# Linear attention and a gated MLP in one kernel: idle products at the start, a held-back turning of q, and tile 0's second layer in another order

## The chip, the core and the metric

The kernel runs on one core of a Trainium2 chip. The metric is the device time of one execution in microseconds (us), lower is better. Each kernel was run three times; the median is shown. Beside those runs stands one execution with the hardware profiler on, whose trace is what is read below.

## The reference

Inputs are q, k, v of shape (8 batches, 8 heads, 576 positions, 64), a norm vector g of 64, w_in (512 x 2048) and w_out (2048 x 512), all float32. The output has 4608 x 512 float32.

```
kv  = einsum('bhsd,bhse->bhde', k, v)
out = einsum('bhsd,bhde->bhse', q, kv)
x   = out / sqrt(mean(out*out, -1) + 1e-6) * g_norm     # attention without softmax, then a norm per head
x   = x.transpose(0, 2, 1, 3).reshape(4608, 512)
h   = x @ w_in
g   = h * (1 / (1 + exp(-1.702 * h)))
y   = g @ w_out
```

## The kernel before, in words

**Tiles.** Each batch gives one tile of 512 rows (positions 0 to 511 of it, or, for the first two batches, 512 of its 576 rows in another numbering). The 64 rows that are left of each batch are collected in `x_rem` and form a ninth tile. The loop at the end of the kernel runs t = 0 to 8: tile t goes through the first layer (x times w_in, with the gate on ScalarE) and the second layer (times w_out), and into the products of tile t the attention of batch t + 1 is woven. `at1(n, ...)` and `at2(n, ...)` put a piece of work behind step n of the tile's first or second layer. Order on every engine is written out by hand (`manual_schedule`); nothing is moved by a scheduler, and every wait follows from the data and the buffers.

**Start.** Before the loop batch 0's attention is done pair of heads by pair of heads (`First`): q turned by TensorE (`q`, 12 narrow products), `kv` (12 narrow products), `out`, `ss` (sum of squares by a product with ones), then a root on ScalarE and `apply` on VectorE. `busy(n)` (L865) issues n products of 128 x 512 into a bank that nobody reads; before, it stands 12, 2 and 2 times among the first pairs. Then tile 0's first layer runs plainly (L473): first the columns 0 to 3 for the parts of w_in, then columns 8 and 9, 10 and 11, 4, 5, 6 and so on (`COLS`).

**Loads.** All loads that change float32 to float16 go through POOL's queue, in the order of the program: k, q, v of batch 0, w_in in eight pieces, then w_out mixed with batch 1's q, k, v (L920 to L930), later batch 2's q (`load_q`), batch 2's k, v in two halves (`load_kv`), and so on. A load is issued only when the load eight places ahead of it in this queue has landed (there are eight semaphores, used in turn), and when the buffer that it writes has been read.

**Tile 0's second layer** (`project_all`, L811) is 64 products of 128 x 512 into four banks o, one for each 128 rows (mo), over 16 row blocks of w_out (fo); two of the banks belong to the first layer's pool of three (`ps_h`). Its list `steps` says which (mo, fo) comes when, and batch 1's attention (`Second`) is woven in by `at2` numbers: q, kv, out, ss, apply for four pairs c. `Second` takes its ss banks from `ps_h`.

**Tiles 1 to 8** use seven products in place of eight for each 2 x 2 block (L584 in the first layer, L704 in the second). This takes sums of weights, made once by VectorE: `w_in_sums` into `ws`, and `weight_sum(n, i0, i1)` (L606) into `tw`, the part n of w_out's sums for row blocks i0 to i1. Products 5, 6, 7 and 4 of the second layer read tw's parts 0, 1, 2 and 3. Sums of the activations go into `xS` and `gS`.

**Turning.** From batch 2 on q and x are turned by DMA, issued from SP's queue: `transpose_q` (qTd, L290), `transpose_rest` (qTr, L294), and two for x (L368). SP's queue also carries the stores of the output: `store_early` (L838), eight stores, for tiles 0 and 1. Before, tile 0's eight stores come first, then batch 2's q.

Of the kernel before, what the change touches and what calls it, by code (L numbers as in the profile page):

```python
# [16 lines left out]
def kernel(  # L17
# [10 lines left out]
    nc = tc.nc  # L28

    B, H, S, D = q.shape  # L30
# [11 lines left out]
    EARLY = 2  # L42
# [47 lines left out]
    def early_load(n, b, c0, c1):  # L90
        nc.gpsimd.dma_start(
            out=raw[n][0:PE_, c0:c1, :].rearrange("p c (l x) -> p (c l) x", l=2),
            in_=early_src(n, b, c0, c1),
        )
# [15 lines left out]
    RS = H * RW  # L110
# [26 lines left out]
    def q_rows(b):  # L137

        rows = qbuf if b % 2 else qraw.rearrange("p c x -> p (c x)")
        return rows[:, 0 : H * J * D]  # L140
# [64 lines left out]
    def load_w_out(f0, f1):  # L205
        nc.gpsimd.dma_start(
            out=w_out_sb[:, f0:f1, :],
            in_=moe_w_out[f0 * P : f1 * P, :].rearrange("(fo ki) n -> ki fo n", ki=P),
        )
# [11 lines left out]
    class Attention:  # L221
# [63 lines left out]
                    r = slice(hl * D, (hl + 1) * D)  # L285
                    copy(self.engine, self.kb[to, c0:c1, half, 1 - hl], self.kvp[r, c0:c1, :])

        def transpose_q(self):
            self.qTd = attn.tile([P, H * J // 2, P], F16, name="qTd", tag="qTd", bufs=1)
            nc.sync.dma_start_transpose(out=self.qTd, in_=q_rows(self.b))  # L290

        def transpose_rest(self):
# [489 lines left out]
    def layers(t, units1, units2):  # L782
        hid = d0 if t == 0 else Hidden(t)
        seven = Seven(t, hid.gT) if t else None
        left = hid_seven(t, hid, seven, units1) if t else first_columns(hid, units1)
        osbs[t] = opool.tile([P, 4, DM], F32, name="osb", tag="osb")
        if t:
            todo = {n: [lambda x=x: seven.sums(*x) for x in xs] for n, xs in plan(t).later.items()}
            for n, us in units2.items():
                todo.setdefault(n, []).extend(us)  # L790
            for n, us in left.items():
                todo[n] = us + todo.get(n, [])
            seven.run(todo)
        else:
            project_all(hid.gT, units2)
        if t < EARLY:
            store_early(t)
        elif t < B and t not in HALVED:
            store(t, 0, J)

    def first_columns(hid, units):
# [9 lines left out]
    def project_all(gT, units):  # L811

        os = {}

        def project(mo, fo):
            if fo == 0:
                pool, tag = (ps_h, "hT") if mo < 2 else (ps_o, "o")
                os[mo] = pool.tile([P, DM], F32, name="o", tag=tag)
            nc.tensor.matmul(  # L819
                os[mo],  # L820
                gT[:, fo, mo * P : (mo + 1) * P],
                w_out_sb[:, fo, :],
                start=(fo == 0),
                stop=(fo == FO - 1),
            )
            if fo == FO - 1:
                copy = nc.scalar.copy if mo % 2 else nc.vector.tensor_copy
                copy(osbs[0][:, mo, :], os[mo])

        steps = [(mo, 4 * i + k) for i in range(3) for mo in range(4) for k in range(4)]  # L830
        steps += [(mo, f + k) for f in (12, 14) for mo in range(2) for k in range(2)]
        steps += [(mo, 12 + k) for mo in (2, 3) for k in range(4)]
        for n, (mo, fo) in enumerate(steps):
            project(mo, fo)
            for u in units.get(n, ()):
                u()
# [52 lines left out]
    a0.ss(0)  # L889
    a0.out(1)  # L890
    a0.q(2)
    a0.kv(2)
    a0.ss(1)
    a0.apply(0)
# [1 line left out]
    a0.q(3)  # L896
    a0.apply(1)
    d0 = Hidden(0)
    a0.kv(3)
    a0.ss(2)  # L900
    a0.apply(2)
# [22 lines left out]
    load_w_out(8, 10)  # L924
    load_w_out(10, 12)
    early_load("v", 1, 0, 2)
    load_w_out(12, 14)
    early_load("k", 1, 2, NPAIR)
    early_load("v", 1, 2, NPAIR)
    load_w_out(14, FO)  # L930

    made = {}
# [49 lines left out]
    for t in range(NT):  # L982
        b = t + 1
        u1, u2 = {}, {}

        def at1(i, f, *args):
            u1.setdefault(i, []).append(lambda: f(*args))

        def at2(i, f, *args):
            u2.setdefault(i, []).append(lambda: f(*args))  # L990

        def of(b, name, *args):
            return lambda: getattr(live[b], name)(*args)

        if t == 0:
            for l in range(2):
                at1(6, nc.vector.memset, kvd[l], 0.0)
            at1(7, of(0, "out", NPAIR))
            at1(7, scale_w_in, 0, 4)
            at1(7, w_in_sums, 0, 2)  # L1000
            at1(8, start, 1)
            at1(12, scale_w_in, 4, 6)
            at1(12, w_in_sums, 2, 3)
            at1(13, load_q, 2)
            at2(4, setattr, a0, "ss_pool", Attention.ss_pool)
            at2(4, of(0, "ss", NPAIR, True))
            at2(4, of(0, "apply", NPAIR))
            at2(18, weight_sum, 0, 0, HF)
            at2(18, scale_w_in, 6, 8)
            at2(18, w_in_sums, 3, 4)  # L1010
            for c in range(NPAIR):
                at1(12, of(1, "pack_q", c))
                at2(9 + 3 * c, of(1, "q", c))
                at2((36, 36, 49, 49)[c], of(1, "kv", c))
                at2((41, 43, 54, 55)[c], of(1, "out", c))
                at2((45, 50, 58, 60)[c], of(1, "ss", c))
                at2((48, 52, 58, 62)[c], of(1, "apply", c))
            for n in range(1, 4):
                at2(19, weight_sum, n, 0, 4)
                at2(38, weight_sum, n, 4, 6)  # L1020
            at2(39, load_kv, 2, 0, H // 2, False)
            at2(51, clear_rest)
            at2(51, load_kv, 2, H // 2, H)

            def first_sum():
                made[1] = Sums(1, xT[1])
                made[1].form(0)

            at2(55, first_sum)
        elif b < B:  # L1030
            todo = plan(t)
            at = todo.attn
            if t == 1:
                at1(todo.steps.index("kv"), of(b, "kv_all", "D"))
                at1(5, start, b)
                at1(5, of(b, "transpose_q"))
                at1(5, of(b, "transpose_rest"))
                at1(4, nc.scalar.preload_act_table_set, "gelu_apprx_sigmoid_and_others")
                for n, i in ((1, 8), (2, 11), (3, 16)):
                    at1(i, weight_sum, n, 6, HF)  # L1040
                at1(22, load_kv, 3)
                at1(22, load_q, 3)
                at2(88, start, 3)
                at2(88, of(3, "kv_all", "A"))
                at2(89, load_kv, 4)
                at2(89, load_q, 4)
            elif t + 2 < B:
                at2(at["rows"][0], start, t + 2)
                at2(at["rows"][0], of(t + 2, "kv_products"))
                at2(52, of(t + 2, "kv_copies", "A"))  # L1050
                if t + 3 < B:
                    at2(at["rows"][0], load_kv, t + 3, 0, H, False, "k")
                    at2(101, after_turn, b)
                    at2(101, load_kv, t + 3, 0, H, True, "v")
                    at2(101, after_queries, t + 2)
                    at2(101, load_q, t + 3)
            if t + 2 < B:
                at2(49 if t > 1 else 100, of(t + 2, "transpose_q"))
                at2(100, of(t + 2, "transpose_rest"))
            at2(at["table"], nc.scalar.preload_act_table_set, "abs_reciprocal_sqrt_and_small")  # L1060
            for h in range(2):
                at2(at["roots"][h], of(b, "roots", h))
            for j in range(J):
                if j < J // 2:
                    at2(at["rows"][j], of(b, "rows", j))
                for name in ("add_up", "turn"):
                    at2(at[name][j], of(b, name, j))
            rest = (80, 90, 96, 97) if 1 < t < B - 2 else (46, 74, 80, 82)
            at2(rest[0], of(b, "out", NPAIR))
            at2(rest[1], of(b, "ss", NPAIR))  # L1070
            at2(rest[2], of(b, "apply", NPAIR))
            at2(rest[3], nc.scalar.preload_act_table_set, "gelu_apprx_sigmoid_and_others")
        elif t < B:
            for name in ("ss_pool", "rest_pool"):
                at2(16, setattr, live[1], name, (ps_a, "att"))
            at2(16, of(1, "out", NPAIR))
            at2(34, nc.scalar.preload_act_table_set, "abs_reciprocal_sqrt_and_small")
            at2(44, of(1, "ss", NPAIR))
            at2(50, of(1, "apply", NPAIR))
            at2(52, nc.scalar.preload_act_table_set, "gelu_apprx_sigmoid_and_others")  # L1080
        layers(t, u1, u2)


# [28 lines left out]
```

## Time and profile before

| what | value |
|---|---|
| median of 3 runs | 259.11 us (258.8 to 259.48) |
| the profiled execution | 259.74 us, of which its span is 258.0 |
| mean granted TensorE clock of that execution | 0.993 |
| TensorE busy (products) | 251.7 us, 98% |
| VectorE busy | 193.9 us, 75% |
| ScalarE busy | 177.1 us, 69% |
| POOL busy (without issuing loads) | 57.0 us, 22% |
| POOL's queue of loads | 18.31 MB, 55.3% of 16 engines' time |
| SP's and ACT's queue | 16.29 MB, 27.4% |

How to read it: the span is from the first to the last recorded instruction; the time of the execution has some 1.7 us around it. PE is TensorE, PEld its loading of weights (which overlaps the products), DVE is VectorE, ACT ScalarE, POOL GpSimd, SP the engine that only issues transfers. A timeline row gives start and length in us, engine, line, operation, what is written and read, shapes, and the count of instructions merged in it; in brackets stands the idle time ahead of it and what ended that. The lengths of products overlap: a row's end lies about 0.17 us behind the start of what follows it without a gap, so distances are taken from start to start. "DMA to landing" is from a transfer's issue to its last byte. A kernel line such as L704 names the call that recorded the instruction, which may be a helper that many places use. In the changed file the lines from 290 on lie two to some ten further down.

### The profile page before, as it was taken

How to read it: one execution, taken by the hardware profiler on the slowest of the kernel's cores; microseconds unless marked ns; L12 is line 12 of the kernel's file. 1: busy time of each engine (PE TensorE's matmuls, PEld its weight loads, DVE VectorE, ACT ScalarE, POOL GpSimd, SP SyncE). 2: the span in 40 equal slices, each digit the busy share in tenths (PEclk: the TensorE clock that was granted, in tenths of full speed). 3: DMA queues.
4: the chain of work that ended last, by engine and by line, in shares of the span. 5: the costliest groups of instructions: out<-in, count | busy, mean ns of one | idle time of the engine just before them, and what ended most of it. 6: DMA issues, size and time to landing. Idle time of an engine off the chain costs nothing.

```text
span 258.0 us, 6355 instructions
## 1 busy us (share of the span) xinstructions
PE 251.7 (98%) x2596; PEld 204.4 (79%) x2596; DVE 193.9 (75%) x344; ACT 177.1 (69%) x322; POOL 57.0 (22%) x92
## 2 busy tenths in 40 slices
PE   8899999999999999999999999999999999999994
PEld 2444454788888888888888888898888888888883
DVE  1546685899958986798679867987799787857872
ACT  3458743988758894899579957995799469536800
POOL 8773244208061013301150134000000000000013
PEclk9979999999999999999999999999999999999999
DMA  7999999999989979996999699909500430012005
GB/s 181 194 188 206 204 204 197 216 216 115 184 159 208 221 91 224 153 158 81 186 184 164 84 205 135 190 5 136 202 4 0 84 163 3 0 57 108 3 19 145
DMA packets 68687, 35.33 MB, mean 137 GB/s; under 512 B 37970, under 2 KB 66258, under 8 KB 68402
## 3 DMA queue, kind: packets, MB, share of 16 engines
q0 software_dynamic: 37632, 18.31, 55.3%
q1 hardware_dynamic: 30624, 16.29, 27.4%
q8 instruction: 20, 0.33, 0.5%
q10 hardware_dynamic: 402, 0.33, 0.5%
q14 instruction: 9, 0.07, 0.1%
HBM read 36.70 MB, written 9.44 MB: 179 GB/s over the span
## 4 chain that ended last, share of the span: by engine, by line
PE 93%; DMA 4%; issue 0%; POOL 0%; DVE 0%
PE o L704 38%; PE h L584 38%; PE hT L473 6%; PE o L819 5%; DMA vbuf<-in_v_dram 2%; DMA qraw<-in_q_dram 2%; PE kvp L247 2%; PE outR L332 1%; PE ss L379 1%; PE outT L302 1%; PE q L454 0%; PE kvp L259 0%; PE outT L306 0%; PE kv L259 0%; DVE osb L684 0%
## 5 line engine op out<-in xcount | busy, mean ns | idle before, releaser
L561 ACT ACTIVATE gT<-h 128x512 f16<-128x512 f32 x96 | 52.5, 601 | 5.6 <-PE h L584 5.6
L584 PEld LDWEIGHTS <-ws 128*128 128x128 f16 x512 | 50.1, 98 | 5.9
L704 PEld LDWEIGHTS <-gS 128*128 128x128 f16 x512 | 49.1, 98 | 6.1 <-DVE gS L636 0.3
L584 PE MATMUL h<-xS,ws 128*128 128x256 f16 x384 | 52.2, 273 | 0.0
L704 PE MATMUL o<-tw,gS 128*128 128x256 f16 x384 | 45.6, 273 | 0.0
L584 PEld LDWEIGHTS <-w_in_sb 128*128 128x128 f16 x384 | 37.4, 98 | 4.7
L704 PEld LDWEIGHTS <-gT 128*128 128x128 f16 x384 | 37.6, 98 | 4.3
L704 PE MATMUL o<-w_out_sb,gT 128*128 128x256 f16 x256 | 31.4, 273 | 0.0
L584 PE MATMUL h<-xT,w_in_sb 128*128 128x256 f16 x224 | 31.1, 272 | 0.0
L681 DVE TENSOR_TENSOR osb<-o,qf 128x512 f32<-128x512 f32 (+1 forms) x25 | 16.7, 669 | 11.7 <-PE o L704 11.7
L598 DVE TENSOR_TENSOR h<-h,s 128x512 f32<-128x512 f32 x32 | 22.2, 698 | 4.2 <-PE h L584 2.6
L600 DVE TENSOR_TENSOR s<-h,s 128x512 f32<-128x512 f32 x32 | 22.1, 691 | 4.1 <-PE h L584 3.3
L738 POOL DMA_DIRECT2D out_dram<-osb x6 | 3.2, 537 | 93.2 <-DVE osb L681 93.2
L636 DVE TENSOR_TENSOR gS<-gT 128x512 f16<-128x512 f16 (+2 forms) x32 | 21.3, 685 | 0.6 <-ACT gT L561 0.6
L561 ACT ACTIVATE gT<-s 128x512 f16<-128x512 f32 x32 | 19.8, 628 | 2.4 <-DVE s L600 2.3
L530 DVE COPY s<-h 128x512 f32<-128x512 f32 x19 | 13.0, 686 | 8.2 <-PE h L584 8.2
L584 PE MATMUL h<-xS,w_in_sb 128*128 128x256 f16 x128 | 18.9, 273 | 0.0
L115 POOL DMA_DIRECT2D kraw<-in_k_dram x7 | 6.0, 853 | 56.9 <-PE kvp L247 52.0
L348 DVE TENSOR_REDUCE sum<-sq 128x8 f32<-128x512 f16 x24 | 14.9, 678 | 4.7 <-ACT sq L342 4.7
L320 ACT ACTIVATE sq<-outT 128x512 f16<-128x512 f32 (+1 forms) x16 | 7.9, 495 | 15.1 <-PE outT L302 9.5
L990 ACT ACT_TABLE_LOAD x14 | 18.0, 1283 | 0.2
L381 ACT ACTIVATE rs<-ss,eps_t 128x512 f32<-128x512 f32 (+1 forms) x16 | 9.2, 582 | 12.4 <-PE ss L379 12.3
(104 smaller groups left out, 373.9 us busy)
## 6 DMA issues: line engine op xcount, KB each, us to landing
out_dram<-osb SPq DMA_DIRECT2D x8, 512.0 KB, 4.6
kraw<-in_k_dram POOLq DMA_DIRECT2D x5, 512.0 KB, 6.0
vbuf<-in_v_dram POOLq DMA_DIRECT2D x5, 512.0 KB, 10.4
out_dram<-osb SPq DMA_DIRECT2D x2, 1024.0 KB, 4.9
qraw<-in_q_dram POOLq DMA_DIRECT2D x3, 512.0 KB, 11.6
qbuf<-in_q_dram POOLq DMA_DIRECT2D x3, 512.0 KB, 10.4
out_dram<-osb SPq DMA_DIRECT2D x6, 192.0 KB, 5.9
w_in_sb<-in_moe_w_in_dram POOLq DMA_DIRECT2D x2, 512.0 KB, 10.1
```

The source lines that it names most:

```text
L348: nc.vector.tensor_reduce(out=self.sum4[:, j, :], in_=self.o[j][1].rearrange("p (x d) -> p x d", d=D), op=ALU.add, axis=mybir.AxisListType.X,)
L473: nc.tensor.matmul(self.h[fo], w_in_sb[:, ko, fo * P : (fo + 1) * P], self.x[:, ko], start=(ko == 0), stop=(ko == KO - 1),)
L530: (nc.vector.tensor_copy if engine == "D" else nc.scalar.copy)(to, src)
L561: nc.scalar.activation(self.gT[:, to, n * TH : (n + 1) * TH], src, AFT.Gelu_apprx_sigmoid)
L584: nc.tensor.matmul(bank[name][:, a], w, x, start=(p in (1, 5) and a == 0 and k == 0), stop=(k == KH - 1), skip_group_check=True,)
L598: nc.vector.tensor_add(bank["z"], bank["x"], self.s5)
L600: nc.vector.tensor_add(self.s5, bank["x"], self.s5)
L636: op(s[:, n, lo], a, b)
L681: nc.vector.tensor_add(o, ps, self.kept[with_][:, m])
L704: nc.tensor.matmul(o, a, w, start=(p in (1, 2, 5) and i == 0 and (mo == 0 or split)), stop=(i == HF - 1), skip_group_check=True,)
L819: nc.tensor.matmul(os[mo], gT[:, fo, mo * P : (mo + 1) * P], w_out_sb[:, fo, :], start=(fo == 0), stop=(fo == FO - 1),)
L990: u2.setdefault(i, []).append(lambda: f(*args))
```

## The change

Seven edits, all in the order of work or in which instruction waits for what; the computation is the same.

1. Four more idle products: `busy(1)` ahead of batch 0's third kv and `busy(3)` ahead of its fourth.
2. Batch 1's last k and v are loaded ahead of w_out's row blocks 12 and 13, and these come in two loads in place of one.
3. The end of tile 0's second layer runs row block 12 for all four mo, then 13 for all four, then 14 and 15 for each mo, and batch 1's kv, out, ss, apply stand at other step numbers. From step 57 on, batch 1 takes its ss banks from the other pool (`ps_a`).
4. w_out's sums: parts 1, 2, 3 of row blocks 4 and 5 are no longer made in tile 0's second layer; parts 1 and 2 of blocks 4 to 7 are made in tile 1's first layer, part 3 of blocks 4 to 7 in tile 1's second layer behind product 80.
5. Tile 2's k, v loads stand behind steps 41 and 54 in place of 39 and 51.
6. Turning batch 2's q waits for a copy of one element by POOL, which reads the last piece of batch 2's v (`transpose_q(after=...)`).
7. Tile 0's eight stores are issued behind the turning of batch 2's q, in tile 1's first layer, in place of at the end of tile 0.

```
-        def transpose_q(self):
+        def transpose_q(self, after=None):
             self.qTd = attn.tile([P, H * J // 2, P], F16, name="qTd", tag="qTd", bufs=1)
+            if after is not None:
+                nc.gpsimd.tensor_copy(out=self.qTd[0:1, 0, 0:1], in_=after)
             nc.sync.dma_start_transpose(out=self.qTd, in_=q_rows(self.b))
...
-        if t < EARLY:
+        if t == 1:
             store_early(t)
-        elif t < B and t not in HALVED:
+        elif 1 < t < B and t not in HALVED:
             store(t, 0, J)
...
         steps = [(mo, 4 * i + k) for i in range(3) for mo in range(4) for k in range(4)]
-        steps += [(mo, f + k) for f in (12, 14) for mo in range(2) for k in range(2)]
-        steps += [(mo, 12 + k) for mo in (2, 3) for k in range(4)]
+        steps += [(mo, fo) for fo in (12, 13) for mo in range(4)]
+        steps += [(mo, 14 + k) for mo in range(4) for k in range(2)]
...
     a0.q(2)
+    busy(1)
     a0.kv(2)
...
     d0 = Hidden(0)
+    busy(3)
     a0.kv(3)
...
     early_load("v", 1, 0, 2)
-    load_w_out(12, 14)
     early_load("k", 1, 2, NPAIR)
     early_load("v", 1, 2, NPAIR)
+    load_w_out(12, 13)
+    load_w_out(13, 14)
     load_w_out(14, FO)
...
             at2(4, setattr, a0, "ss_pool", Attention.ss_pool)
+            at2(57, lambda: setattr(live[1], "ss_pool", Attention.ss_pool))
...
-                at2((36, 36, 49, 49)[c], of(1, "kv", c))
-                at2((41, 43, 54, 55)[c], of(1, "out", c))
-                at2((45, 50, 58, 60)[c], of(1, "ss", c))
-                at2((48, 52, 58, 62)[c], of(1, "apply", c))
+                at2((40, 40, 47, 47)[c], of(1, "kv", c))
+                at2((44, 45, 51, 54)[c], of(1, "out", c))
+                at2((47, 48, 56, 58)[c], of(1, "ss", c))
+                at2((50, 52, 57, 60)[c], of(1, "apply", c))
             for n in range(1, 4):
                 at2(19, weight_sum, n, 0, 4)
-                at2(38, weight_sum, n, 4, 6)
-            at2(39, load_kv, 2, 0, H // 2, False)
-            at2(51, clear_rest)
-            at2(51, load_kv, 2, H // 2, H)
+            at2(41, load_kv, 2, 0, H // 2, False)
+            at2(54, clear_rest)
+            at2(54, load_kv, 2, H // 2, H)
...
-                at1(5, of(b, "transpose_q"))
+                at1(5, of(b, "transpose_q", kv_rows["v"][0:1, RS + H * D - 1 : RS + H * D]))
                 at1(5, of(b, "transpose_rest"))
+                at1(5, store_early, 0)
                 at1(4, nc.scalar.preload_act_table_set, "gelu_apprx_sigmoid_and_others")
-                for n, i in ((1, 8), (2, 11), (3, 16)):
-                    at1(i, weight_sum, n, 6, HF)
+                for n, i in ((1, 8), (2, 11)):
+                    at1(i, weight_sum, n, 4, HF)
+                at2(80, weight_sum, 3, 4, HF)
```

## The prediction

> **What bounds the kernel now.** I read the page's chain of waits and clock line first, then TensorE's windows and timeline at the start, then single loads with their time to landing, then the stretches that the change touches.
>
> ```profile
> span 258.0 us, 6355 instructions
> PE 93%; DMA 4%; issue 0%; POOL 0%; DVE 0%
> PEclk9979999999999999999999999999999999999999
> ```
>
> The chain that ended last is TensorE for 93% of the span; the rest is loads ahead of it. The clock line falls in one slice of 40, the third (12.9 to 19.4 us). So only two things can be won: TensorE's waits, and the slow clock of that slice. The windows of TensorE alone (us, busy, granted clock, DMA share, GB/s) cut it finer:
>
> ```profile
> 3.06:6.47 3.41, 3.41 (x9) 1.00 1.13 240
> 6.47:9.88 3.41, 3.03 (x59) 1.00 1.28 190
> 9.88:13.29 3.41, 2.51 (x40) 1.00 1.27 196
> 13.29:16.70 3.41, 3.41 (x20) 0.51 1.31 180
> ```
>
> After a window that was 2.51 of 3.41 us busy comes one at clock 0.51; after 3.03 of 3.41 it did not fall. The DMA share is above 1 throughout: loads set the pace beside TensorE. TensorE's timeline there (start, length, count, wait before it):
>
> ```profile
> 1.28 5.30 PE L867 MATMUL idle<-kvb 128*128 128x512 f16 x12 [1.28 <-DVE one_t L202]
> 9.02 0.45 PE L434 MATMUL q<-ident,qraw 96*64 96x96 f16 x12
> 9.30 0.35 PE L259 MATMUL kv<-vbuf,kraw 96*64 96x64 f16 x12
> 10.54 0.45 PE L434 MATMUL q<-ident,qraw 96*64 96x96 f16 x12
> 11.09 0.38 PE L259 MATMUL kv<-vbuf,kraw 96*64 96x64 f16 x12
> 13.29 0.50 PE L259 MATMUL kv<-vbuf,kraw 96*64 96x64 f16 x12 [0.68 <-DMA vbuf<-in_v_dram]
> 15.40 1.71 PE L473 MATMUL hT<-xT,w_in_sb 128*128 128x512 f16 x4
> 17.17 5.78 PE L473 MATMUL hT<-xT,w_in_sb 128*128 128x512 f16 x26
> 22.90 7.07 PE L473 MATMUL hT<-xT,w_in_sb 128*128 128x512 f16 x32
> 29.81 1.24 PE L819 MATMUL o<-w_out_sb,gT 128*128 128x512 f16 x5
> 47.80 0.60 PE L584 MATMUL h<-xT,w_in_sb 128*128 128x256 f16 x4
> ```
>
> A 512-wide product takes 0.216 us at full clock ((29.81 - 22.90) / 32) and 0.43 when slow (1.71 / 4). From 17.17 on there is hardly a gap.
>
> **Four idle products.** One stands before batch 0's third kv, three before its fourth; 4 x 0.216 = 0.86 us of work. Twelve q products issue in 0.28 (9.02 to 9.30), so the third kv at 11.09 follows a hole of 11.09 - 10.54 - 0.28 = 0.27, and the fourth one of 0.68 or more, in which it waits for v. One product (0.22) and three (0.65) fit in. Their cost is 0; bounds 0 and +0.86, the latter if the loads behind those holes came at once, which nothing here suggests. They raise the window at 9.88 from 2.51 to about 3.2 busy of 3.41, above the 3.03 that kept the clock. I take it that the clock stays.
>
> What that is worth: the fourth kv (0.28) and the 15 wide products after it, up to the first that needs w_in's columns 8 and 9, end at 13.29 + 0.28 + 15 x 0.216 = 16.8, with small waits for w_in's first quarter and a copy 17.0. Before, that product stood at 17.17 + 6 x 0.216 = 18.47 (six of the 26 come ahead of it). So up to 1.45 could be won, but the loads do not move. Two of them, with the third row for the v load:
>
> ```profile
> L180 POOL DMA_DIRECT2D w_in_sb<-in_moe_w_in_dram x1: 747/747/747, 10.5 to 10.5; - x1
> DMA to landing us min/median/max: 7.0/7.0/7.0
> ...
> L180 POOL DMA_DIRECT2D w_in_sb<-in_moe_w_in_dram x1: 747/747/747, 12.8 to 12.8; - x1
> DMA to landing us min/median/max: 9.2/9.2/9.2
> ...
> 7.59 5.57 DMA vbuf<-in_v_dram
> ```
>
> v lands at 13.16 and its product starts 0.13 later (13.29). Columns 8 and 9 land at 17.5, so their product starts at 17.63. Twenty wide products (4.33) and four narrow ones (0.11) later, at 22.07, TensorE wants columns 4 to 7, which land at 12.75 + 9.2 = 21.95, usable at 22.08. Before, it began them at 22.90. **Term: -0.82**; bounds 0 (the clock falls all the same) and -1.45 (the loads come sooner).
>
> A rule of the Trainium skill speaks against this term: "TensorE: Matmul & The Clock Gate", section "Why this matters for your kernels", asks only that no idle gap between bursts exceeds about 3 us. By it the holes of 0.27 and 0.68 would not matter and the term would be 0; the trace disagrees so far, with clock 0.51 behind holes no longer than 0.68.
>
> **Batch 1's loads, steps and w_out.** Tile 0's second layer has the same 64 products. It runs from 29.81 to 47.80, 17.99 us; its work is 64 x 0.216 plus 3.9 of attention products, 17.75, so it holds 0.24 of waits. The rows that set them now and after:
>
> ```profile
> 41.04 1.25 ACT L320 ACTIVATE sq<-outT 128x512 f16<-128x512 f32 x2 [5.15 <-PE outT L302]
> 41.92 0.38 PE L379 MATMUL ss<-sq,ones 128*128 128x512 f16 x1
> 42.33 0.69 ACT L381 ACTIVATE rs<-ss,eps_t 128x512 f32<-128x512 f32 x1
> ...
> L206 POOL DMA_DIRECT2D w_out_sb<-in_moe_w_out_dram x1: 705/705/705, 24.7 to 24.7; - x1
> DMA to landing us min/median/max: 14.6/14.6/14.6
> ...
> L91 POOL DMA_DIRECT2D vbuf<-in_v_dram x1: 673/673/673, 30.1 to 30.1; - x1
> DMA to landing us min/median/max: 11.9/11.9/11.9
> ```
>
> From ss to the end of its root are 42.33 + 0.69 - 41.92 = 1.10. Two first-layer banks are held by rows of o, so batch 1's second ss needs the first's root done; after the change only kv's 0.50 and two products (0.43) stand between the two, so it waits 0.2. The last ss takes a bank of the other pool and does not wait. Waits of 0.2 replace waits of 0.24: **term 0**, bounds -0.2 and +0.4.
>
> The loads: w_out's rows 12 and 13 landed at 24.74 + 14.6 = 39.3 and batch 1's last v at 30.14 + 11.9 = 42.0. With k and v put ahead, each comes 1.3 sooner (the gap that the pair of rows filled) and row 12 lands at about 41.5. TensorE wants the last k, v at 29.0 + 12.7 = 41.7 and row 12 at 42.2, counted from its new start of the layer (29.81 - 0.82). Both are there, by 0.9 and 0.5; if a load slips past, the wait is up to 0.5. POOL's queue issues each load when the one eight places ahead has landed, and splitting the pair of rows adds one place: tile 2's q goes out 0.9 later, but the queue never runs dry, so nothing behind it lands later.
>
> **VectorE's sums and the gS wait.**
>
> ```profile
> 64.21 0.77 PEld L704 LDWEIGHTS <-gS 128*128 128x128 f16 x8 [0.27 <-DVE gS L636]
> ...
> L612 DVE TENSOR_TENSOR tw<-w_out_sb,tw 128x1024 f16<-128x1024 f16 x2 | 1.4, 689 | 0.1
> ```
>
> Six sums of 0.42 become three of 0.69. Two stand in tile 1's first layer (1.38 instead of three of 0.42, 1.26), one in its second layer at product 80, in a hole of VectorE of 1.5 us, and 1.3 ahead of the product that reads it. Batch 1's last two applies end about 1 us earlier against the layer's end, so VectorE comes to gS some 0.15 ahead, and of the wait of 0.27 a part goes: **term -0.08**, bounds -0.15 and +0.15. If VectorE's lead is lost, it pays the extra 0.12 there.
>
> **q's turning and tile 0's stores held back.** A POOL copy now waits for tile 2's last v piece; SP's turning of q waits for the copy, and behind it in SP's queue stand the small turning and tile 0's eight stores, behind these x's turnings of tile 2.
>
> ```profile
> 46.27 4.38 SPq L843 DMA_DIRECT2D out_dram<-osb  x8
> 51.40 4.26 SPq L290 DMA_TRANSPOSE qTd<-qraw  x1
> 63.26 0.64 PE L332 MATMUL outR<-kvd,qTd 64*128 64x64 f16 x32
> 71.86 0.82 PE L247 MATMUL kvp<-vbuf,kraw 128*64 128x64 f16 x40
> ...
> 58.00:60.00 2.00, 2.00 (x20) 1.79 (x19) 1.93 (x6) 1.76 (x4) 1.76 (x2) 1.00 0.09 13
> ...
> L120 POOL DMA_DIRECT2D vbuf<-in_v_dram x1: 691/691/691, 60.8 to 60.8; - x1
> DMA to landing us min/median/max: 7.2/7.2/7.2
> ```
>
> Without the stores' 4.38 among them, tile 2's loads land by about 52; turning starts there, against 51.40, and takes at most 4.26 plus 1.2 for the small one: done by 58, wanted at 63.26 - 0.9. The stores then issue from 56 to 62, partly in the stretch where the DMA share is 0.09 now. The copy holds nothing up on POOL: the load behind it waits for tile 2's kv anyway. Beside the stores run tile 3's k, v, whose last piece landed at 60.8 + 7.2 = 68.0 and is wanted at 71.86: 3.9 to spare. **Term 0**; bounds 0 and +2, worked out below.
>
> **Sum.** -0.82 + 0 + 0 - 0.08 + 0 = -0.90. The profiled execution took 259.74 (span 258.0 and 1.74 around it): 258.84. It is 0.63 above the median of the runs, 259.11, to which I apply the same -0.90: **258.2 us**.
>
> **Rivals.**
> (1) The clock falls as before, because holes this short do not decide it, or the median run never lost what the profiled one did. For it: one window is all that I have, 2.51 against 3.03 busy is a thin bound, the wide products of 1.28 (5.30 / 12 = 0.44 each) were slow for 5 us under full busy, so the clock goes by windows whose place I cannot set; and the runs spread over 258.8 to 259.48, as far as this term. Then only -0.1 to -0.3 is left: 258.9. The Trainium skill (the page named above, section "Part 1: The HAM clock gate") gives a window of 3413 ns that runs free of the kernel's start; the slow stretch of 3.41 agrees.
> (2) The loads come sooner than here, since TensorE's two waits for w_in are all that is left: -1.45 - 0.1, 257.6. Against it: their queue is full from the first microsecond.
> (3) Slower: turning and stores, both moved behind tile 2's loads, meet tile 3's k, v. If those slip by more than 3.9, TensorE stands at the kv of 71.86. The stores alone are 4.38 of issue, and with the 4.26 of turning they are 8.6; halfway between 4.4 and 8.6 the slip is 6.5, some 2 more than is spare after the earlier start: -0.9 + 2 = +1.1, 260.2. Against it: the idle stretch at 58 to 60, and turning that is quicker without loads beside it.
>
> **How the numbers follow.** What a measurement of this kernel can tell from no change is 0.3%, 0.78 us: faster is below 258.33, slower above 259.89. The forecast has 0.57, with a range of its own from 257.9 to 258.6, about 0.47 of it below 258.33 and 0.10 above. Rival 1 has 0.24 (no change), rival 2 0.08 (faster), rival 3 0.11 (slower). So faster 0.55, same 0.34, slower 0.11. The range runs from rival 2's 257.6 to 259.4, which holds rival 1 with the spread of the runs, and leaves out rival 3 and the edges.
>
> **What would show it.** Clock near 1.00 in the window of 13.29 to 16.70; the 26 products split by a wait for w_in before columns 8, and the 32 starting at about 22.1; the second layer starting near 29.0 and lasting 18.0; TensorE's kv of tile 3 at about 71.0 with no wait before it. Wrong if the clock still shows 0.5 there, if w_out's row 12 or batch 1's v ends a wait in the layer, or if the kv near 71 waits for a load.

## The result, and the profile after

The changed kernel is slower: 262.25 us (median of 6 runs, 261.31 to 262.75) against 259.30 us of the kernel before beside it (median of 6, 258.75 to 260.17). The ratio is 1.0107, with a 95% interval from 1.0085 to 1.0129. Ratios here leave out a run that took over 1.5% more than the fastest of its kernel, which are two of the twelve of stores_back and none elsewhere. The prediction said 258.2 us, with a range that ended at 259.4.

The page of the execution profiled after (262.03 us) begins like this; the last two rows are groups of the first layer's products, with their busy time, the mean ns of one, and the idle time before them:

```profile
span 260.2 us, 6364 instructions
PEclk9999999999999999999999999999999999999999
PE 91%; DMA 6%; DVE 1%; SPq 0%; issue 0%; DVEq 0%
L586 PE MATMUL h<-xS,ws 128*128 128x256 f16 x384 | 52.4, 273 | 1.2 <-DVE xS L514 1.1
L586 PE MATMUL h<-xT,w_in_sb 128*128 128x256 f16 x224 | 31.0, 273 | 1.9 <-DMA xT<-x 1.9
```

The dip of the clock line is gone, and yet the span is 2.2 us longer. DMA has grown from 4% to 6% of the chain that ended last, and the first layer's products now wait 1.9 for `xT<-x`, a name that stood in no row of the prediction: x's turning by DMA. The start went better than forecast. First the windows at 9.88 and 13.29, here with all engines (length, then busy time and in brackets the count of PE, PEld, DVE, ACT and POOL, then granted clock, DMA share, GB/s), then TensorE's timeline:

```profile
9.88:13.29 3.41, 3.21 (x43) 1.51 (x43) 2.02 (x5) 2.33 (x4) 2.98 (x5) 1.00 1.28 198
13.29:16.70 3.41, 3.41 (x27) 1.66 (x27) 1.63 (x4) 2.12 (x4) 3.20 (x5) 1.00 1.33 190
```

```profile
10.59 0.39 PE L869 MATMUL idle<-kvb 128*128 128x512 f16 x1
12.56 0.82 PE L869 MATMUL idle<-kvb 128*128 128x512 f16 x3
13.32 0.38 PE L259 MATMUL kv<-vbuf,kraw 96*64 96x64 f16 x12
21.55 7.07 PE L475 MATMUL hT<-xT,w_in_sb 128*128 128x512 f16 x32
28.46 1.24 PE L821 MATMUL o<-w_out_sb,gT 128*128 128x512 f16 x5
46.47 0.60 PE L586 MATMUL h<-xT,w_in_sb 128*128 128x256 f16 x4
...
70.58 0.82 PE L247 MATMUL kvp<-vbuf,kraw 128*64 128x64 f16 x40
72.11 1.91 PE L706 MATMUL o<-tw,gT 128*128 128x256 f16 x16
75.91 1.92 PE L586 MATMUL h<-xT,w_in_sb 128*128 128x256 f16 x16 [1.89 <-DMA xT<-x]
78.97 1.67 PE L586 MATMUL h<-xS,ws 128*128 128x256 f16 x12 [1.13 <-DVE xS L514]
```

The four idle products fit where they were put, and the kv behind them moved by 0.03 (13.29 to 13.32). The 32 products start 1.35 earlier (22.90 to 21.55), tile 0's second layer lasts 18.01 against 17.99, and at tile 3's kv TensorE is still 1.28 ahead (71.86 to 70.58), with no wait there. TensorE's rows of the profile before from there to tile 4's kv, and that kv after:

```profile
73.39 1.91 PE L704 MATMUL o<-tw,gT 128*128 128x256 f16 x16
75.14 1.92 PE L584 MATMUL h<-xT,w_in_sb 128*128 128x256 f16 x16
76.89 1.36 PE L584 MATMUL h<-xS,ws 128*128 128x256 f16 x11
89.21 0.82 PE L247 MATMUL kvp<-vbuf,kraw 128*64 128x64 f16 x40
```

```profile
91.48 0.82 PE L247 MATMUL kvp<-vbuf,kraw 128*64 128x64 f16 x40
```

The lead of 1.28 has become a lag of 2.27 at tile 4's kv. Tile 2's first layer followed the 16 products of 73.39 after 1.75 us; now it follows those of 72.11 after 3.80, and its first products on xS, VectorE's sums of the turned x, come 3.06 behind its start instead of 1.75. That is 2.05 + 1.31 = 3.36 of the 1.28 + 2.27 = 3.55, and both waits hang on the two turnings of x.

SP's queue before the change, with x's turnings for tile 2 and the turning of tile 3's q behind them, and the time of x's turnings to landing:

```profile
68.74 3.26 SPq L368 DMA_TRANSPOSE xT<-x  x2
72.17 1.92 SPq L290 DMA_TRANSPOSE qTd<-qbuf  x1
...
L368 SPq DMA_TRANSPOSE xT<-x x2: 1232/1586/1939, 68.7 to 70.1; - x2
DMA to landing us min/median/max: 4.0/4.2/4.5
```

The same of after, with POOL's copy (edit 6, called the hold from here on). The last rows are the load of tile 3's q, of after and then of before:

```profile
52.49 0.18 POOL L291 COPY qTd<-vbuf 1x1 f16<-1x1 f16 x1 [5.88 <-DMA vbuf<-in_v_dram]
52.70 1.78 SPq L292 DMA_TRANSPOSE qTd<-qraw  x1
56.46 6.34 SPq L845 DMA_DIRECT2D out_dram<-osb  x8
67.46 5.81 SPq L370 DMA_TRANSPOSE xT<-x  x2
...
L370 SPq DMA_TRANSPOSE xT<-x x2: 1267/2856/4446, 67.5 to 68.8; - x2
DMA to landing us min/median/max: 8.4/9.0/9.6
...
L143 POOL DMA_DIRECT2D qbuf<-in_q_dram x1: 902/902/902, 60.5 to 60.5; - x1
DMA to landing us min/median/max: 13.8/13.8/13.8
...
L143 POOL DMA_DIRECT2D qbuf<-in_q_dram x1: 902/902/902, 61.4 to 61.4; - x1
DMA to landing us min/median/max: 9.2/9.2/9.2
```

x's turning is issued 1.28 earlier, as everything is, but takes 8.4 and 9.6 us to land instead of 4.5 and 4.0. Tile 3's k, v, q are loaded from 56.92 on, and the stores of tile 0, 1 MB, now run beside them. The last of the large ones, q, landed at 60.53 + 13.8 = 74.3; before, it was issued at 61.4 and landed after 9.2, at 70.6. So in the new order x's turning has loads beside it until nearly its own end. They are not its only neighbours: the last stores, issued by 62.3, land by 69.4, and tile 4's loads are issued from 71.67, where before they went out at 72.95, when the first turning had all but landed. Windows of before, and below them of after (columns as above), show where room was given up and where it was taken:

```profile
52.00:54.00 2.00, 2.00 (x21) 1.79 (x19) 2.00 (x5) 1.81 (x4) 0.00 (x0) 1.00 1.47 335
72.00:74.00 2.00, 2.00 (x53) 1.82 (x50) 0.49 (x2) 1.44 (x5) 1.05 (x2) 1.00 1.16 255
```

```profile
52.00:54.00 2.00, 2.00 (x20) 1.70 (x19) 2.00 (x5) 1.84 (x4) 0.18 (x1) 1.00 0.01 2
72.00:74.00 2.00, 2.00 (x19) 1.57 (x16) 0.69 (x1) 0.94 (x3) 2.00 (x3) 1.00 1.64 117
74.00:76.00 2.00, 0.11 (x2) 0.09 (x2) 0.00 (x0) 0.59 (x1) 2.00 (x4) 1.00 1.39 160
```

From 52 to 54 the DMA engines now stand nearly still (share 0.01 where it was 1.47): tile 2's last v has landed at 45.93 + 6.5 = 52.4, and q's turning, which the hold lets go at 52.70, moves next to nothing before 54. From 74 to 76 they are busy and TensorE works for 0.11 of 2 us.

### The profile page after: what moved, and what is told of

Same layout as the page of the kernel before. It is cut to its first block, busy times and chain, and to the rows that moved or that the text cites. A ratio compares the mean times of both kernels' runs of the same rounds, so it can differ in the third digit from the quotient of the medians.

```text
span 260.2 us, 6364 instructions
## 1 busy us (share of the span) xinstructions
PE 251.6 (97%) x2600; PEld 204.0 (78%) x2600; DVE 194.3 (75%) x341; ACT 177.1 (68%) x322; POOL 57.5 (22%) x94
## 4 chain that ended last, share of the span: by engine, by line
PE 91%; DMA 6%; DVE 1%; SPq 0%; issue 0%; DVEq 0%
PE h L586 37%; PE o L706 36%; PE hT L475 5%; PE o L821 5%; DMA xT<-x 4%; DMA qf<-in_v_dram 2%; PE kvp L247 1%; PE outR L334 1%; PE ss L381 1%; PE outT L304 1%; PE idle L869 1%; PE q L436 0%; PE kv L259 0%; PE q L456 0%; PE kvp L259 0%; SPq L161 0%
## 5 line engine op out<-in xcount | busy, mean ns | idle before, releaser
L586 PE MATMUL h<-xS,ws 128*128 128x256 f16 x384 | 52.4, 273 | 1.2 <-DVE xS L514 1.1
L532 ACT COPY h<-h 128x512 f32<-128x512 f32 x27 | 15.4, 576 | 4.0 <-PE h L586 3.8
```

The costliest lines, as they stand in the source:

```text
L532: (nc.vector.tensor_copy if engine == "D" else nc.scalar.copy)(to, src)
L586: nc.tensor.matmul(bank[name][:, a], w, x, start=(p in (1, 5) and a == 0 and k == 0), stop=(k == KH - 1), skip_group_check=True,)
```

## The experiments

The main theory was A: the hold and the new place of the stores put the stores beside tile 3's loads, these land later, and x's turning, which then runs beside them, becomes slow. Theory B was that any earlier start of TensorE runs into x's turning. Nine kernels were tried, in three groups; each group had its own runs of the kernel before, with medians of 258.89, 258.88 and 258.92 us.

**stores_back.** The changed kernel with tile 0's stores at the end of tile 0 again, the hold kept.

```
-        if t == 1:
+        if t < EARLY:
             store_early(t)
...
-                at1(5, store_early, 0)
```

> The changed kernel with tile 0's eight stores back at the end of tile 0, ahead of q's turning; the hold on that turning stays. Theory A (the stores, pushed behind the turning to 56.5 to 62.8 us, delay tile 3's k, v and q loads, and x's turning for tile 2 then runs beside these): x's turning lands in 4 to 5 us in place of 8.4 and 9.6, TensorE does not wait at tile 2's start, the span is about 3.3 us below the 260.2 of the changed kernel, and the time about 258.5. Theory B (TensorE is 1.3 us ahead while the transfers are not, so any faster start runs into the turning): a wait of 1 us or more stays there and the time is 259.5 to 260.5.

Measured: 260.18 us (258.77 to 263.21, 12 runs), ratio 1.0038 (1.0010 to 1.0065). In its profile the last load of tile 3, q, lands at 70.9, x's turning takes 6.3 and 7.6, and TensorE waits for VectorE's sums alone, 1.2. Most of the loss goes with the stores; something stays, and differs much from run to run. So theory A's forecast (4 to 5 us, 258.5) was missed, and the time is in theory B's range. The profile shows one likely reason: with the stores beside tile 2's loads, its v lands at 55.5, the hold lets q's turnings go only at 55.71, and these run beside tile 3's loads (issued from 56.78), whose q takes 10.5 to land in place of 9.2.

**no_hold.** The changed kernel without the hold: the stores stay behind q's turnings in SP's queue.

```
-                at1(5, of(b, "transpose_q", kv_rows["v"][0:1, RS + H * D - 1 : RS + H * D]))
+                at1(5, of(b, "transpose_q"))
```

> The changed kernel without the hold: q's turning for batch 2 waits for q alone; the stores still stand behind it. Theory A: turning goes out near 46 us, the stores at about 48 to 54, before tile 3's loads begin at 56.9, and x's turning lands in 4 to 5 us; time about 258.5. Theory C (the stores standing directly ahead of x's turning in SP's queue are what slows it, whenever they are issued): x's turning stays at 7 us or more and the time near 261.5. Theory B: 259.5 to 260.5.

Measured: 258.88 us (258.16 to 259.99), ratio 0.9993 (0.9976 to 1.0009). The stores are issued from 51.88 to 56.6, ahead of tile 3's loads (the last lands by 60, beside them), and no product waits for x's turning (5.3 and 5.8 to landing, where theory A said 4 to 5); one wait of 0.7 is left, for tile 4's v. So it is not the stores' place in the queue, directly ahead of x's turning, that costs (theory C): that place is the same here.

**idle_alone.** The kernel before with the four idle products alone (edit 1).

```
     a0.q(2)
+    busy(1)
     a0.kv(2)
...
     d0 = Hidden(0)
+    busy(3)
     a0.kv(3)
```

> The kernel before with the four idle products and nothing else. Theory A: the clock stays at 1.00 from 13.3 to 16.7 us, the second layer of tile 0 starts 0.8 to 1.35 us earlier, and since nothing else moves the gain is kept: 258.0 to 258.5. Theory B: the layer starts as much earlier, but the gain is lost in a wait for transfers by tile 2's start: 259.0 to 259.5.

Measured: 258.75 us (258.50 to 259.45, 12 runs), ratio 0.9987 (0.9968 to 1.0005): within what can be told from no change. The profile shows the gain of the start in full (the second layer begins at 28.44, against 29.81), and no product waits at tile 2's start, so theory B does not hold here. Yet the median hardly moves. The clocks say why: of the 65 runs of the kernel before in the three groups, only 4, all in the first group, have a mean granted clock of 0.993, the one of the profile that the prediction read; they took 259.40 to 260.18. The other 61 stand at 0.997 or more, with the median at 258.89. A window of 3.41 us at clock 0.51 costs 3.41 x 0.49 / 258 = 0.0065 of the span's mean, which is about what 0.993 stands for; in which stretch those four lost it is not on record. So the prediction's term describes a loss that few runs have.

**hold_stores_alone.** The kernel before with the hold and the moved stores alone (edits 6 and 7; the copy inside `transpose_q` as in the change).

```
-        if t < EARLY:
+        if t == 1:
             store_early(t)
...
-                at1(5, of(b, "transpose_q"))
+                at1(5, of(b, "transpose_q", kv_rows["v"][0:1, RS + H * D - 1 : RS + H * D]))
                 at1(5, of(b, "transpose_rest"))
+                at1(5, store_early, 0)
```

> The kernel before with the hold on q's turning and the stores behind it, and nothing else. Theory A: the same wait at tile 2's start as in the changed kernel, 3.3 us, with no gain ahead of it: about 262.5. Theory B: TensorE is not ahead, so the wait is 1.3 us less, about 2 us, and the time 261.

Measured: 261.91 us (261.23 to 262.77, 6 runs), ratio 1.0110 (1.0086 to 1.0135): the whole loss, between the two forecasts. x's turning takes 8.6 and 9.3. TensorE's timeline there, and its windows:

```profile
28.08 1.24 PE L821 MATMUL o<-w_out_sb,gT 128*128 128x512 f16 x5
75.80 3.29 PE L586 MATMUL h<-xT,w_in_sb 128*128 128x256 f16 x16 [2.11 <-DMA xT<-x]
...
9.88:13.29 3.41, 2.22 (x51) 1.38 (x50) 2.34 (x5) 2.07 (x4) 2.95 (x6) 1.00 1.29 202
13.29:16.70 3.41, 3.41 (x25) 1.50 (x18) 1.67 (x4) 2.41 (x4) 2.93 (x4) 1.00 1.35 192
76.00:78.00 2.00, 2.00 (x12) 1.41 (x11) 0.09 (x1) 0.57 (x1) 0.60 (x1) 0.54 1.47 198
```

Two things are to be seen. Without the idle products the start is as fast as with them: the clock stays at 1.00 although the window at 9.88 is only 2.22 busy, and the second layer begins at 28.08. So this kernel was as early as the changed one, and the run does not tell theory A from B. And the clock falls in another place, behind the wait of 2.11 for x's turning, where 16 products take 3.29 in place of 1.92.

**edits_1_to_5.** The changed kernel with both edits undone, the hold and the stores.

```
-        if t == 1:
+        if t < EARLY:
             store_early(t)
...
-                at1(5, of(b, "transpose_q", kv_rows["v"][0:1, RS + H * D - 1 : RS + H * D]))
+                at1(5, of(b, "transpose_q"))
...
-                at1(5, store_early, 0)
```

> The changed kernel with the hold on q's turning undone and tile 0's stores back at the end of tile 0: what is left are the idle products, batch 1's loads and steps, w_out's sums and tile 0's second layer. If the hold and the moved stores carry the whole loss (two runs with the one or the other gave 1.0038 and 0.9993, and the two alone on the kernel before 1.011), this is at the kernel before or a little under it: 258.3 to 259.2 us, ratio 0.996 to 1.001, x's turning for tile 2 landing in 4 to 5.5 us, and no wait at tile 2's first layer. Rival: part of the loss comes from the other edits, so that they give a few tenths back: above 259.5 us.

Measured: 258.76 us (258.12 to 259.30, 12 runs), ratio 0.9999 (0.9988 to 1.0011), inside the forecast. The rest of the change gains and costs nothing that can be measured. In the profile the second layer begins at 28.11, as early as in the changed kernel, and nothing waits for x's turning (4.7 and 4.2): theory B is out.

**stores_last.** The changed kernel with the hold kept and the stores behind both of x's turnings.

```
-                at1(5, store_early, 0)
...
                     at2(at[name][j], of(b, name, j))
+            if t == 1:
+                at2(53, store_early, 0)
```

> The changed kernel with the hold kept and tile 0's eight stores moved once more, behind both of x's turnings for tile 2 in SyncE's queue. Theory A1 (the hold is half of it, the stores the other half: each pushes the loads of tile 3 back by its own bytes and so under x's turning): q's load of tile 3 lands near 71 as it did with the stores at tile 0's end (70.9), x's turning lands in 5 to 7.6 us, TensorE waits under 0.8 us for it, 259 to 260.4 us. Theory A2 (the hold alone does it, wherever the stores are): turning 8 us or more and 261.5 us or more. Rival (a new queue jam): the stores behind the turning issue from about 72 and hold tile 3's q turning, behind them, to 78 or later, so that a wait appears in tile 2's or 3's attention that no run so far had: above 260.4 us with x's turning quick.

Measured: 260.72 us (259.72 to 263.37, 8 runs), ratio 1.0084 (1.0046 to 1.0122). x's turning is quick (4.2 and 4.3) and nothing waits for it, so the hold alone does not slow it here. The loss has moved, in the way of the third rival: SP's queue, then TensorE further on:

```profile
70.93 4.91 SPq L845 DMA_DIRECT2D out_dram<-osb  x8
75.95 7.67 SPq L292 DMA_TRANSPOSE qTd<-qbuf  x1
...
90.27 0.64 PE L334 MATMUL outR<-kvd,qTd 64*128 64x64 f16 x32 [1.09 <-DMA qTd<-qbuf]
```

The stores hold back the next turning, that of tile 3's q, which then runs beside tile 4's loads (issued from 71.56): it takes SP's queue 7.67 us where it took 1.92 before, and lands too late. The three longest runs, 262.20 to 263.37, are those with a mean clock of 0.993.

**q3_behind_turn.** The changed kernel, with tile 3's load of q, and so tile 4's loads behind it on POOL, waiting for x's turning.

```
-                at1(22, load_q, 3)
...
                     at2(at[name][j], of(b, name, j))
+            if t == 1:
+                at2(53, after_turn, b)
+                at2(53, load_q, 3)
```

> The changed kernel, hold and moved stores kept, with one thing added: tile 3's load of q, and with it tile 4's loads behind it in GpSimd's queue, wait until x's turning for tile 2 has landed, so that beside the turning there is only the end of tile 3's k and v. Theory A (the loads that run beside x's turning make it slow): the turning lands in 4 to 6 us instead of 8.4 and 9.6, TensorE's wait for it falls from 1.9 us (with 1.1 for the sums behind it) to under 0.6 in all, and the time comes down from 262.3 to 258.8 to 260 us, unless tile 3's q or tile 4's k and v then come too late further on, which would show as a wait of their own after 85 us. Theory D (the turning is late because of what is ahead of it, the stores or the attention): still 8 us or more, 261.5 us or more.

Measured: 262.71 us (261.68 to 264.26, 6 runs), ratio 1.0150 (1.0119 to 1.0181). Half of theory A's forecast came: the turning takes 5.5 and 5.9 in place of 8.4 and 9.6, and no product waits for it. It had the stores beside it (the last, issued at 63.6, lands by 70.8) and not tile 3's q nor tile 4's loads, so it is these, together, that make up most of the slowing; the run does not tell q from tile 4's loads. The time did not come down (the profiled execution is the longest of the six, 264.26, at a clock of 0.993):

```profile
71.69 0.32 PE L247 MATMUL kvp<-vbuf,kraw 128*64 128x64 f16 x8 [0.84 <-DMA vbuf<-in_v_dram]
72.67 0.69 PE L247 MATMUL kvp<-vbuf,kraw 128*64 128x64 f16 x32 [0.67 <-DMA vbuf<-in_v_dram]
91.87 0.69 PE L247 MATMUL kvp<-vbuf,kraw 128*64 128x64 f16 x32 [1.65 <-DMA vbuf<-in_v_dram]
93.10 1.03 PE L334 MATMUL outR<-kvd,qTd 64*128 64x64 f16 x32 [0.54 <-DMA qTd<-qbuf]
```

Tile 3's k and v are still beside the stores and land last at 72.6, and tile 4's loads, put off, are late at 91.87. That second wait the forecast had named as its exception, the first it had not: with the stores in that stretch, putting off one transfer moves the wait to another.

**stores_held.** The hold is taken off q's turning and put on the stores, by a copy of one element in SP's queue that reads tile 2's kv.

```
-                at1(5, of(b, "transpose_q", kv_rows["v"][0:1, RS + H * D - 1 : RS + H * D]))
+                at1(5, of(b, "transpose_q"))
-                at1(5, store_early, 0)
...
+                at1(22, lambda: nc.sync.dma_start(out=mark2, in_=live[2].kb[0:1, 0, 0, 1, 0:1]))
+                at1(22, store_early, 0)
                 at1(22, load_kv, 3)
```

> The changed kernel with the hold taken off q's turning and put on tile 0's stores instead: q's two turnings issue at 45 and 50 us as without a hold, and the eight stores wait in SyncE's queue, behind one copy of a single element, until VectorE has written tile 2's kv, near 56.5 us, when tile 3's loads start too. Theory S (what costs is the 1 MB of stores running beside tile 3's loads, the hold is only what put them there): tile 3's q lands at 73 us or later, x's turning in 7.5 us or more, TensorE waits 1 to 3.5 us before tile 2's first layer, 260.8 to 262.5 us. Theory H (it takes q's two late turnings too, and the stores alone can be borne there): q lands before 72, x's turning within 6 us, no wait above 0.5 us, 258.3 to 259.8 us.

Measured: 262.05 us (261.62 to 262.60, 6 runs), ratio 1.0113 (1.0094 to 1.0132), theory S. SP's queue, TensorE and x's turning:

```profile
45.71 5.03 SPq L293 DMA_TRANSPOSE qTd<-qraw  x1
57.97 5.89 SPq L846 DMA_DIRECT2D out_dram<-osb  x8
76.22 3.21 PE L587 MATMUL h<-xT,w_in_sb 128*128 128x256 f16 x16 [2.17 <-DMA xT<-x]
...
L371 SPq DMA_TRANSPOSE xT<-x x2: 1278/2959/4640, 67.5 to 68.9; - x2
DMA to landing us min/median/max: 8.7/8.7/8.7
```

q's turnings are early, as before the change, and only the stores run beside tile 3's loads: all of the loss is there. Against no_hold it is the time of the stores that differs (issued from 57.97 in place of 51.88, behind the one-element copy), and the ratio goes from 0.9993 to 1.0113.

**stores_end.** The hold kept, tile 0's stores at the end of tile 1, ahead of tile 1's own.

```
         if t == 1:
+            store_early(0)
             store_early(t)
...
-                at1(5, store_early, 0)
```

> The changed kernel with the hold kept and tile 0's stores moved to the end of tile 1, ahead of tile 1's own: from 45 to 75 us SyncE's queue holds nothing but q's held turnings, x's turning and tile 3's q turnings. Theory S (the stores beside tile 3's loads are the loss): q of tile 3 lands near 70 us, x's turning in 4 to 6 us, no wait before tile 2's first layer nor, as it came with the stores behind x's turning, at tile 3's q, 258.3 to 259.5 us. Theory H (the held turnings themselves run beside tile 3's loads and cost, as the 1.0038 with the stores at tile 0's end suggests): x's turning 6 to 8 us in many of the executions, 259.6 to 261 us with a spread of 2 us or more.

Measured: 259.65 us (258.94 to 260.32, 12 runs), ratio 1.0023 (1.0009 to 1.0037): just inside theory H's range, but with the turning that theory S said, and its spread of 1.4 is less than theory H asked. x's turning:

```profile
L370 SPq DMA_TRANSPOSE xT<-x x2: 1233/1686/2139, 68.2 to 69.5; - x2
DMA to landing us min/median/max: 4.1/4.2/4.3
```

That is the time of before, with the hold in place; a wait of 0.8 for tile 4's v is left, beside 16 stores that are issued from 75.96 to 88.5. So the hold does x's turning no harm here, where q's turning goes at 53.32, nor in stores_last, where it goes at 52.45; in stores_back, where the stores do not run beside tile 3's loads either but q's turning goes at 55.71, x's turning was slow. Whether the 0.0023 is the hold's or the later stores' was not told apart.

The runs in one table (stores against tile 3's loads, which start near 57; x's two turnings from issue to landing in the profiled execution, the shorter first; and how long after the issue of the first the last large load of tile 3 lands, which is q, and v in q3_behind_turn):

| kernel | stores issued | x's turning | loads run on for | ratio to before |
|---|---|---|---|---|
| before | 46.3 to 50.7 | 4.0, 4.5 | 1.9 | 1 |
| idle_alone | 45.0 to 49.4 | 4.5, 4.5 | 1.8 | 0.9987 |
| edits_1_to_5 | 45.5 to 50.7 | 4.2, 4.7 | 1.8 | 0.9999 |
| no_hold | 51.9 to 56.6 | 5.3, 5.8 | 4.1 | 0.9993 |
| stores_back | 45.7 to 50.4 | 6.3, 7.6 | 3.6 | 1.0038 |
| stores_end | 76.0 to 88.5 | 4.1, 4.3 | 2.2 | 1.0023 |
| stores_last | 70.9 to 75.8 | 4.2, 4.3 | 1.5 | 1.0084 |
| after | 56.5 to 62.8 | 8.4, 9.6 | 6.9 | 1.0107 |
| hold_stores_alone | 56.4 to 62.9 | 8.6, 9.3 | 7.0 | 1.0110 |
| stores_held | 58.0 to 63.9 | 8.7, 8.7 | 7.1 | 1.0113 |
| q3_behind_turn | 56.6 to 64.1 | 5.5, 5.9 | 5.0 | 1.0150 |

x's turning goes with the fourth column: 4.0 to 4.7 us where the loads run on for 1.5 to 2.2, 5.3 to 7.6 for 3.6 to 5.0, 8.4 to 9.6 for 6.9 to 7.1. Inside the middle group the order does not hold, so this is not all; there q3_behind_turn is the one without tile 4's loads beside the turning. All kernels with a ratio above 1.01 issue the stores beside tile 3's loads, and no other kernel does. None of the versions beats the kernel before by more than the noise.

## Why the prediction was wrong

**The step that failed** is the term of q's turning and tile 0's stores, "Term 0; bounds 0 and +2". Its pieces held: q's turning started at 52.70 where 52 was said, and the stores issued from 56.46 to 62.8, "from 56 to 62". What failed is the one wait against which it was tested. I asked whether tile 3's last v comes by its kv, with 3.9 to spare; it came at 59.86 + 10.6 = 70.5, for a kv at 70.58, so 2.5 of slip and 1.3 of earlier start used the 3.9 up almost exactly and nothing was paid. But v is not the last of these loads: q comes behind it, landing at 74.3, and x's turning, issued from the very queue that the stores were moved in, runs beside it. I had named "x's turnings of tile 2" as standing behind the stores and gave them no duration, no due time and no row. In the profile before they took 4.0 to 4.5 us with loads beside them until 70.6; the first landed at 68.74 + 4.5 = 73.2, for a layer that started at 75.14. The spare was 1.9 us, not 3.9, and the two turnings slowed by 3.9 and 5.6. Measured, the term was +3.55 in the profiled execution, from the lead of 1.28 to the lag of 2.27, and +3.0 on the median (hold_stores_alone, 261.91 against 258.89): above its bound of +2.

**Rival 3** was the right neighbourhood (turning and stores meet tile 3's loads, slower) with the wrong wait, and its price too low: 260.2 against 262.25. Its sum does not come out either: a slip of 6.5 less the 3.9 to spare is 2.6, not 2, and 3.5 if the earlier start of 0.9 is taken off what is spare, which makes 260.8 or 261.7. That the latter is near would be luck, since v slipped by 2.5, not 6.5. Stores and q's turnings as one lump of 8.6 us were its reason; stores_held shows that the stores do it without the turnings, and no_hold that 5 us earlier they cost nothing that can be measured.

**The four idle products.** In the profiled execution they cost nothing and the clock held, as forecast, and the start came earlier by more than forecast: -1.35 against -0.82, near the bound of -1.45. But that the products held the clock is not shown: hold_stores_alone has none of them, kept the clock there and began its second layer at 28.08, where edits_1_to_5 with them began at 28.11. The loads that I held fixed came sooner, as in rival 2: the 32 products began at 21.55, before the 22.08 at which I let their columns be usable (both w_in loads landed 0.4 sooner after their issue, 6.6 and 8.8). On the median the same term is some -0.1 (idle_alone, not told from nothing), which is the second half of rival 1: "the median run never lost what the profiled one did". I had the sign of it in hand, a profile 0.63 above its own median with clock 0.993, and put the full -0.90 on the median all the same. That was a second wrong step, by itself worth 0.8; with the +3.0 of the first it makes 258.2 + 0.8 + 3.0 = 262.0, against 262.25 measured.

**My reading of the clock** was wrong as well. I took 2.51 busy of 3.41 as what let the clock fall and 3.03 as enough; hold_stores_alone kept the clock at 1.00 behind 2.22, in a window whose edges are, like those of before, my own choice. What lets the clock fall stays open. The Trainium skill, "TensorE: Matmul & The Clock Gate", section "What's actually happening", says that the window runs free of the kernel and that one kernel therefore differs from run to run; 4 runs of 65 at 0.993 agree. The rule of its section "Why this matters for your kernels", no idle gap above about 3 us between bursts, was not enough here: the clock fell to 0.54 behind a wait of 2.11.

**What held at its size.** Batch 1's loads, steps and w_out: term 0, and the layer lasted 18.01 (18.0 said). (64 x 0.216 + 3.9 is 17.72, so the layer's waits before were 0.27, not 0.24; nothing hung on it.) The gS term: -0.08 was said; the wait of 0.27 is there unchanged, so it was 0, inside its bounds. edits_1_to_5, at 0.9999, agrees with both.

## What to carry to other kernels

When a transfer is moved, list every transfer that is then in flight with it and, for each, what waits for its landing: price the one with the least spare time, not the one whose wait is already visible. Idle DMA time in one stretch is no reason to move work there if the stretch behind it is full. And compare the profiled execution with the median of the runs before costing anything: what only that execution loses cannot be won on the median.

## What was not expected of the hardware

A DMA turning of x of 128 x 1024 elements landed in 4.0 to 4.5 us while tile 3's loads ended by 70.6, and in 8.4 to 9.6 when they ended at 74.3; with that q and tile 4's loads put behind it, in 5.5 to 5.9. q's turnings vary too: batch 2's kept SP's queue for 1.78 us in the changed kernel, where the DMA share was 0.01, and for 4.26 before, where it was 1.47; tile 3's took 1.92 before and 7.67 in stores_last. The share alone does not tell: it was 1.16 at that 1.92 (72 to 74) and 1.02 to 1.25 in most of the 7.67 (76 to 82). Plain loads beside the stores grew by less in proportion, v's last piece from 7.2 to 10.6 and q from 9.2 to 13.8, but they had other neighbours than the turning, so these rows do not show that a turning suffers more than a load; the reason was not looked for.

A wait of 2.1 us in the middle of full work can cost more than itself: in two of the profiles (waits of 2.11 and 2.17) the 16 products behind it took 3.29 and 3.21 us in place of 1.92, in the first at a granted clock of 0.54, while behind 1.89 in the changed kernel's own profile the clock held. In q3_behind_turn the three runs at a mean clock of 0.993 took 263.54 to 264.26 us, the three at 1.00 took 261.68 to 261.88.
